# First head group of a fused attention and MLP kernel: two query quarters take their heads in pairs, four tokens load on ScalarE's queue, queries are made three units ahead, two Wo tiles move to empty MLP slots

## The chip, the cores and the metric

The kernel runs on one core of one Trainium2 chip. A core has TensorE (PE, with its weight loads as PEld), VectorE (DVE), ScalarE (ACT), GpSimd (POOL) and SyncE (SP), each with its own instruction queue; DMA transfers are issued from SP, ACT and POOL. The metric is device microseconds of one execution; lower is better.

## The reference

The input x (2048 tokens, 512 wide) is layer-normalised. One branch is attention with 32 heads of 128 against given key and value caches, the other a gated MLP; the result is x + s * silu(B).

```python
xn = _layernorm(x, axis=-1)
# A: attention
q = (xn @ wq).reshape(B, Sq, H, Dh)            # 32 heads of 128
scores = einsum("bhqd,bhkd->bhqk", q, k_cache) * (Dh ** -0.5)
p = softmax(scores)
s = einsum("bhqk,bhkd->bhqd", p, v_cache) @ wo
# B: MLP
h = gelu(_layernorm(xn) @ w1)
hs = shift_quarters(h) @ w2                    # four column quarters moved by 1, -1, 2, -2 tokens
x1 = xn + hs
g = silu(x1 + gelu(_layernorm(x1) @ w3) @ w4)
out = x + s * g
```

## The kernel before

The 2048 tokens are 16 tiles of 128, or four quarters (qt) of 512. The 32 heads are eight groups (g) of four (hh). A *unit* is one head of one quarter, 128 in all, in the order of the list `units` (line 121): group, then quarter, then head. A unit has eight *steps*; step p of unit u has the number n = 8u + p. The loop from line 695 writes out the order of every engine by hand (`pin` keeps program order):

- `s_slot` (line 183): two score matmuls into one of two buffers `ps_s`, and one exp of 128x1024 on ACT into `pT`.
- `pv_slot` (line 212), five steps later: two matmuls of `pT` with values into `ps_o`.
- `q_mm` and `q_copy` (lines 167, 175): the four matmuls of the query projection of unit u + 2, in steps 0 and 1, and their copy to `qT` on DVE in step 2 (on ACT in the last units).
- DVE adds the exps of a unit into `acc` (`add_first`, `add_next`, `add_last`); `sums` (line 223) reduces it with four narrow matmuls in step 3 of the next unit; the reciprocal goes through DRAM (`dr`) and is broadcast (`rb`) by two SP DMAs; `norm` (line 253) scales `ps_o` into `oT` in step 2 of the unit after that.
- When the four heads of a quarter are done, `wo_todo` gets its four token tiles. One tile a unit: four Wo matmuls in steps 4 and 5 and a DVE add into `s_acc` in step 6.
- The MLP is cut into 136 *chunks* of mostly four matmuls. Steps 2, 3 and 6, 7 are its windows, two a unit, from unit 5 on; a count spreads the chunks evenly, so that some windows stay empty. The first chunks (`gelu_chunk`) put on ACT a PSUM copy each, and a square and a tanh for each pair.

PSUM has two small banks besides: `xa` (queries, sums, Wo) and `xm` (MLP chunks; the sums of the last seven units).

Before the loop, tokens 0 to 3 are normalised, turned on TensorE and copied to `xnT`, two of three ACT copies first, and the first query made (`first_tokens`, line 377). `xnT` for tokens 4 to 15 is made beside the loop: load on POOL's queue (`ln1_load`), statistics on DVE with a root on POOL (`ln1_stats`), normalisation on DVE (`ln1_apply`), and a transposing DMA on SP (`ln1_turn`). The table `tokens` (line 661) gives the step of each. Keys come by transposing DMAs on SP, four pieces a head (`load_k`), values in two halves (`load_v`). DMAs of SP and ACT share eight completion counters, which a scheduler gives out in turn; a DMA whose counter is still held by an earlier one waits on its engine's queue.

Of the kernel before, what the change touches and what calls it, by code (L numbers as in the profile page):

```python
# [10 lines left out]
FP32 = mybir.dt.float32  # L11
# [6 lines left out]
def kernel(  # L18
# [15 lines left out]
    nc = tc.nc  # L34
# [4 lines left out]
    Sq, D = x2d.shape  # L39
# [78 lines left out]
        pin(nc.gpsimd.tensor_scalar(out=ve[:], in0=var, scalar1=EPS, scalar2=None, op0=ALU.add))  # L118
        pin(nc.gpsimd.tensor_tensor(out=out, in0=ve[:], in1=nhalf[:], op=ALU.pow))

    units = [(g, qt, hh) for g in range(NG) for qt in range(QT) for hh in range(HG)]
    NU = len(units)
    QUIET = NU - 7
    LQ = QT - 1
    deferred = {(NG - 2, qt): qt for qt in (LQ - 1, LQ)}
    NS = NU * SPU
    kTs, vBs, wqs, wos, oTs, st = {}, {}, {}, {}, {}, {}
# [2 lines left out]
    def at(n, fn):  # L130
        todo[n].append(fn)
# [6 lines left out]
    def evict(n):  # L138
        return n if n % SPU == SPU - 1 else n + 1

    def load_k(h, pieces):
        w = Sk // KSPLIT
        for i in pieces:
            if i == 0:
                kTs[h] = kp.tile([P, Sk], BF16, name="kT")
            pin(nc.sync.dma_start(
                out=kTs[h][:, i * w:(i + 1) * w],
                in_=A_k_cache[0, h, i * w:(i + 1) * w, :], transpose=True))
# [14 lines left out]
    def load_wo(h):  # L163
        wos[h] = wop.tile([P, D], BF16, name="wo_h")
        pin(nc.sync.dma_start(out=wos[h][:], in_=A_wo[h * Dh:(h + 1) * Dh, :]))

    def q_mm(u, dcs):
        g, qt, hh = units[u]
        if dcs[0] == 0:
            st[u] = dict(psq=psX.tile([P, 512], FP32, tag="xm" if u == HG else "xa", name="ps_q"))  # L170
        for dc in dcs:
            mm(st[u]["psq"][:], wqs[g * HG + hh][:, dc, :],
               xnT[:, dc, qt * 512:(qt + 1) * 512], dc == 0, dc == DC - 1)

    def q_copy(u):
        qT = qtp.tile([P, 512], BF16, name="qT")
        if u > QUIET + 1:
            pin(nc.scalar.activation(out=qT[:], in_=st[u].pop("psq")[:], func=ACT.Identity))
        else:
            pin(nc.vector.tensor_copy(out=qT[:], in_=st[u].pop("psq")[:]))  # L180
        st[u]["qT"] = qT
# [40 lines left out]

    def sums(u):
        s = st[u]
        ps = psX.tile([P, 4], FP32, tag="xa" if u + 1 < QUIET else "xm", name="ps_sum")
        a = s["acc"][:, 0, :].rearrange("k (p j) -> k j p", j=4)
        for j in range(4):
            mm(ps[:, j:j + 1], a[:, j, :], ones_t[:], True, True)
        recip(s, ps)
# [36 lines left out]
    def wo_mm(g, t, hhs):  # L266
        if hhs[0] == 0:
            wo_box[0] = psX.tile([P, D], FP32, tag="xa", name="ps_wo")
        held = g == NG - 1 and (NG - 2, t // 4) in deferred
        if held and hhs[0] == 0:  # L270
            wo_part(wo_box[0][:], g - 1, t, range(HG), True, False)
        wo_part(wo_box[0][:], g, t, hhs, hhs[0] == 0 and not held, hhs[-1] == HG - 1)

    def wo_part(ps, g, t, hhs, first, last):
        oT = oTs[(g, t // 4)]
        ts = t % 4
        for hh in hhs:
            mm(ps, oT[:, hh, ts * P:(ts + 1) * P], wos[g * HG + hh][:],
               first and hh == hhs[0], last and hh == hhs[-1])
# [61 lines left out]
    def ln1_load(t, eng):  # L341
        xin = tokp.tile([P, D], BF16, tag="ta", bufs=8, name="xin")
        pin(eng.dma_start(out=xin[:], in_=xsrc[t]))
        ln[t] = xin
# [21 lines left out]
    def ln1_apply(t):  # L366
        xns[t] = ln1_norm(t)

    def ln1_turn(t):
        pin(nc.sync.dma_start_transpose(out=xnT[:, :, t * P:(t + 1) * P], in_=xns.pop(t)[:]))  # L370
# [273 lines left out]
        ln1_load(t, eng)  # L644
    act1 = const.tile([P, 1], FP32, name="act1")
    pin(nc.scalar.activation(out=act1[:], in_=nhalf[:], func=ACT.Identity))
    for h in range(HG - 1):
        load_w(h, nc.gpsimd)
    load_k(0, range(KSPLIT))
# [3 lines left out]
    for t in range(4):  # L653
        ln1_stats(t)
    load_w(HG - 1, nc.gpsimd)
    for t in range(4, 8):
        ln1_load(t, nc.gpsimd)
    first_tokens()
    load_v(1, (0, 1))
    load_k(2, (0, 1))  # L660
    tokens = ((2, 4, 5), (5, 9, 12), (8, 12, 13), (11, 14, 14),
              (21, 27, 27), (23, 29, 29), (29, 35, 35), (35, 39, 39),
              (39, 45, 45), (47, 53, 53), (55, 61, 61), (63, 69, 69))
    for t, (stats, apply, turn) in enumerate(tokens, 4):
        if t >= 8:
            at(stats - 8, lambda t=t: ln1_load(t, nc.gpsimd))
        at(stats, lambda t=t: ln1_stats(t))
        at(apply, lambda t=t: ln1_apply(t))
        at(turn, lambda t=t: ln1_turn(t))
    for n, h, piece in ((2, 2, 2), (4, 2, 3), (12, 3, 0), (15, 3, 1), (17, 3, 2), (20, 3, 3)):  # L670
        at(n, lambda h=h, piece=piece: load_k(h, (piece,)))
    for n, h, half in ((7, 2, 0), (13, 2, 1), (20, 3, 0), (21, 3, 1)):
        at(n, lambda h=h, half=half: load_v(h, (half,)))
    at(28, ph1_load)
    at(64, w2_load)
    for h in range(HG):
        at(31 + h, lambda h=h: load_wo(h))
    for g in range(NG - 1):
        b = (g * QT + QT - 1) * HG
        for hh in range(HG):  # L680
            h = (g + 1) * HG + hh
            for i in range(KSPLIT):
                at((b - 2 + (2 * hh + i // 2 + (hh > 0))) * SPU + (5, 7)[i % 2], lambda h=h, i=i: load_k(h, (i,)))
            for i in range(2):
                at((b - 2 + (2 * hh + i + (hh > 0))) * SPU + 6, lambda h=h, i=i: load_v(h, (i,)))
            at((b + (-4, -4, -1, -1)[hh]) * SPU + (5, 7)[hh % 2], lambda h=h: load_w(h))
            at((b - 4 - hh // 2) * SPU + (5, 7)[hh % 2], lambda h=h: load_wo(h))

    at(QUIET * SPU, tail_open)
    for t in range(4 * LQ, NT):  # L690
        if t % 4 < 2:
            at((QUIET + 1 + 2 * (t % 4)) * SPU + 4, lambda t=t: gate_sum(t))

    wo_todo = deque()
    for n in range(NS):
        u, p = divmod(n, SPU)
        s_slot(u, p)
        m = n - LAG
        if m >= 0:
            pv_slot(*divmod(m, SPU))  # L700
        if u == 0 and p in (1, 3, 5):
            q_mm(1 + p // 2, range(DC))
        if u == 0 and p in (2, 4, 6):
            q_copy(p // 2)
        if u == HG - 2 and p in (6, 7):
            q_mm(HG, (2 * p - 12, 2 * p - 11))
        if u == HG - 2 and p == 7:
            q_copy(HG)
        if p in (0, 1) and HG - 1 <= u < NU - 2:
            q_mm(u + 2, (2 * p, 2 * p + 1))  # L710
        if p == 0 and u >= 1:
            add_last(u - 1)
        if p == 2 and HG - 1 <= u < NU - 2:
            q_copy(u + 2)
        if p == 2 and u >= 2:
            norm(u - 2)
            gg, qq, hh = units[u - 2]
            if hh == HG - 1 and (gg, qq) in deferred:
                pin(nc.sync.dma_start(out=o_d[qq][:], in_=oTs[(gg, qq)][:]))
            elif hh == HG - 1:  # L720
                wo_todo.extend((gg, 4 * qq + ts) for ts in range(4))
                if gg == NG - 1:
                    fin_load(4 * qq)
        if p == 3 and u >= 1:
            sums(u - 1)
        if p == 4 and u >= 1:
            bcast(u - 1)
        if p in (4, 5) and wo_todo:
            wo_mm(*wo_todo[0], (0, 1) if p == 4 else (2, 3))
        if p == 6 and QUIET <= u < NU - 1:  # L730
            add_next(u, 2)
        if p == 6 and wo_todo:
            gg, t = wo_todo.popleft()
            wo_post(gg, t)
            if gg == NG - 1:
                at(n + 5, lambda t=t: wo_out(t))
                if t % 4 < 3:
                    fin_load(t + 1)
        if p == 4:
            add_first(u)  # L740
        if p == 4 and u == NU - 1:
            a = st[u]["acc"]
            pin(nc.vector.tensor_tensor(out=a[:, 0:2, :], in0=a[:, 0:2, :], in1=a[:, 2:4, :], op=ALU.add))
        if p == 6 and u < QUIET:
            add_next(u, 2)
        if p in (2, 3, 6, 7):
            w = 2 * u + (p >= 4)
            i = p % 2
            if i == 0:
                want = -(-(w + 1 - W0) * NCH // (W1 - W0)) if w >= W0 else 0  # L750
                window.pop("run", None)
                if done < min(want, NCH):
                    if done in hooks:
                        hooks.pop(done)(n)
                    window["run"] = chunks.popleft()
                    done += 1
            if "run" in window:
                window["run"](i, n)
        for fn in todo.pop(n, ()):
            fn()  # L760
# [78 lines left out]
```

## Time and profile before

| what | value |
|---|---|
| median of 3 runs | 1279.92 us (1279.73 to 1281.28) |
| profiled execution, its time | 1279.53 us |
| its span, first to last instruction | 1277.8 us |
| exps (ACT, 128x1024), one after another | 0.92 us each (15 in 13.86 us) |
| first score matmul | 10.29 us |
| units 1 to 4 (18.92 to 52.75) | 33.83 us |
| units 5 to 12 (52.75 to 133.24) | 80.49 us |
| transposing DMAs of keys, issue to landing, median | 4.7 us |
| transposing DMAs of `xnT`, issue to landing, median | 3.8 us |

Times in the text are microseconds from the start of the span unless they are durations. A unit's window runs from its first exp to the next unit's first exp. Matmul ends are modelled in the profile, so the pitch of matmuls is read from their starts and from whole units. A row of the timeline has start, duration, engine, line, operation and tiles, and in brackets the idle time before it and what ended it; a row of the waits has total, times and longest.

### The profile page before, as it was taken

The numbers are of one execution on the slowest core, as the hardware profiler recorded it, in microseconds if no ns is written. First come the engines' busy times: TensorE is split into PE (matmuls) and PEld (weight loads), VectorE is DVE, ScalarE is ACT, GpSimd is POOL, SyncE is SP. The second block draws the span as 40 slices with busy tenths as digits, with TensorE's granted clock in tenths as the row PEclk, the third lists the DMA queues.
The fourth block names the chain that finished last, engine by engine and source line by source line (L and its number), as shares of the span: only waits on it lengthen the run. The fifth ranks groups of instructions, "written<-read, shape, count | busy, mean of one in ns | idle before, by whom it ended". The sixth has DMA issues, their size and how long they took to land.

```text
span 1277.8 us, 17233 instructions
## 1 busy us (share of the span) xinstructions
PE 1257.1 (98%) x6195; PEld 612.1 (48%) x6320; DVE 1019.2 (80%) x1407; ACT 1113.0 (87%) x1195; POOL 137.9 (11%) x241
## 2 busy tenths in 40 slices
PE   8999999999999999999999999999999999999998
PEld 5444444444444444444444444444444444444444
DVE  7888889898788877778887778887777888777886
ACT  7899998888999988899988889998888999888883
POOL 4430003323110010000001000000000000000110
PEclk9999999999999999999999999999999999999999
DMA  9644343455532564134443244523435133542532
GB/s 185 133 106 81 59 79 88 108 124 123 115 77 67 100 110 89 42 75 83 89 93 68 58 85 93 96 42 75 96 80 90 34 70 72 91 105 46 140 76 58
DMA packets 172950, 111.79 MB, mean 87 GB/s; under 512 B 124800, under 2 KB 149888, under 8 KB 172864
## 3 DMA queue, kind: packets, MB, share of 16 engines
q1 hardware_dynamic: 163904, 85.51, 34.3%
q0 software_dynamic: 8672, 24.91, 7.9%
q8 instruction: 49, 0.80, 0.3%
q14 instruction: 37, 0.30, 0.1%
q10 hardware_dynamic: 288, 0.26, 0.1%
HBM read 82.58 MB, written 7.60 MB: 71 GB/s over the span
## 4 chain that ended last, share of the span: by engine, by line
PE 87%; ACT 6%; DVE 4%; issue 1%; DMA 1%; POOL 0%; DVEq 0%; ACTq 0%
PE ps_s L114 31%; PE ps_o L114 30%; PE ps_m L114 9%; PE ps_wo L114 8%; PE ps_q L114 7%; ACT pT L194 4%; PE ps_sum L114 1%; ACT sq L425 1%; DVE acc L205 1%; ACT pre L455 1%; DVE bn L349 0%; DMA rb<-dr 0%; DMA xnT<-xn 0%; DVE acc L210 0%; DVE qT L180 0%
## 5 line engine op out<-in xcount | busy, mean ns | idle before, releaser
L194 ACT ACTIVATE pT<-ps_s 128x1024 bf16<-128x1024 f32 x1024 | 1012.0, 1031 | 141.0 <-PE ps_s L114 130.0
L114 PE MATMUL ps_s<-qT,kT 128*128 128x512 bf16 x2004 | 599.5, 379 | 4.1 <-ACT pT L194 1.0
L114 PE MATMUL ps_o<-pT,vb 128*128 128x512 bf16 x1997 | 597.6, 379 | 2.8
L205 DVE TENSOR_TENSOR acc<-acc,pT 128x2048 bf16<-128x2048 bf16 x254 | 309.8, 1220 | 65.5 <-ACT pT L194 60.8
L114 PEld LDWEIGHTS <-kT 128*128 128x128 bf16 x2048 | 226.8, 113 | 224.4 <-issue 18.6
L114 PEld LDWEIGHTS <-vb 128*128 128x128 bf16 x2048 | 199.8, 98 | 225.2
L200 DVE TENSOR_TENSOR acc<-pT 128x2048 bf16<-128x2048 bf16 x128 | 155.9, 1218 | 26.6 <-ACT pT L194 26.4
L114 PE MATMUL ps_q<-xnT,wq_h 128*128 128x512 bf16 (+1 forms) x519 | 150.7, 374 | 3.3 <-DMA xnT<-xn 2.0
L114 PE MATMUL ps_wo<-wo_h,oT 128*128 128x512 bf16 x456 | 136.3, 379 | 0.6
L328 DVE TENSOR_TENSOR s_acc<-ps_wo,s_acc 128x512 f32<-128x512 f32 x100 | 68.9, 689 | 73.9 <-PE ps_wo L114 71.0
L210 DVE TENSOR_TENSOR acc<-acc 128x1024 bf16<-128x1024 bf16 x127 | 87.9, 692 | 4.4
L261 DVE TENSOR_TENSOR oT<-ps_o,rb 128x512 bf16<-128x512 f32 x129 | 87.1, 676 | 4.1 <-DMA rb<-dr 4.0
L180 DVE CAST qT<-ps_q 128x512 bf16<-128x512 f32 x122 | 83.5, 685 | 4.8 <-PE ps_q L114 4.8
L114 PEld LDWEIGHTS <-wq_h 128*128 128x128 bf16 x524 | 50.6, 98 | 63.2 <-issue 3.6
L114 PEld LDWEIGHTS <-oT 128*128 128x128 bf16 x480 | 46.9, 98 | 57.7 <-issue 2.6
L114 PE MATMUL ps_m<-xn2T,w_sb 128*128 128x512 bf16 x222 | 66.1, 378 | 0.2
L114 PE MATMUL ps_m<-w_sb,h2T 128*128 128x512 bf16 x218 | 62.7, 379 | 0.2
L577 POOL DMA_DIRECT2D w_sb<-in_B_w_dram x28 | 21.1, 756 | 353.8 <-PE ps_m L114 328.6
L211 DVE TENSOR_TENSOR acc<-acc 128x512 bf16<-128x512 bf16 x127 | 54.0, 425 | 4.3
L233 DVE RECIPROCAL rc<-ps_sum 128x4 f32<-128x4 f32 x128 | 22.9, 179 | 40.9 <-PE ps_sum L114 40.0
L114 PEld LDWEIGHTS <-acc 128*128 128x128 bf16 x516 | 37.6, 115 | 29.6 <-issue 1.5
L609 POOL DMA_DIRECT2D g_d<-xr x16 | 8.8, 547 | 346.3 <-DVE xr L607 346.3
(74 smaller groups left out, 599.9 us busy)
## 6 DMA issues: line engine op xcount, KB each, us to landing
rb<-dr SPq DMA_DIRECT2D x128, 256.0 KB, 4.1
vb<-in_A_v_cache_dram SPq DMA_DIRECT2D x64, 256.0 KB, 4.5
w_sb<-in_B_w_dram POOLq DMA_DIRECT2D x28, 256.0 KB, 4.6
wo_h<-in_A_wo_dram SPq DMA_DIRECT2D x32, 128.0 KB, 3.9
wq_h<-in_A_wq_dram SPq DMA_DIRECT2D x28, 128.0 KB, 4.2
kT<-in_A_k_cache_dram SPq DMA_TRANSPOSE x128, 4.7
dr<-rc SPq DMA_DIRECT2D x128, 2.0 KB, 1.4
xr<-in_A_x_dram POOLq DMA_DIRECT2D x16, 128.0 KB, 3.5
```

The source lines that it names most:

```text
L114: pin(nc.tensor.matmul(out=out, lhsT=lhsT, rhs=rhs, start=start, stop=stop))
L180: pin(nc.vector.tensor_copy(out=qT[:], in_=st[u].pop("psq")[:]))
L194: pin(nc.scalar.activation(out=s["pT"][-1][:, jj:jj + 2, :], in_=sps[:], func=ACT.Exp, scale=SCALE))
L200: pin(nc.vector.tensor_tensor(out=s["acc"][:], in0=s["pT"][0][:], in1=s["pT"][1][:], op=ALU.add))
L205: pin(nc.vector.tensor_tensor(out=a[:], in0=a[:], in1=st[u]["pT"][i][:], op=ALU.add))
L210: pin(nc.vector.tensor_tensor(out=a[:, 0:2, :], in0=a[:, 0:2, :], in1=a[:, 2:4, :], op=ALU.add))
L211: pin(nc.vector.tensor_tensor(out=a[:, 0, :], in0=a[:, 0, :], in1=a[:, 1, :], op=ALU.add))
L233: pin(nc.vector.reciprocal(out=rc[:], in_=ps[:]))
L261: pin(nc.vector.tensor_tensor(out=oTs[(g, qt)][:, hh, c], in0=s["o"][:, c], in1=s["rb"][:, c], op=ALU.mult))
L328: pin(nc.vector.tensor_tensor(out=sa, in0=ps[:], in1=sa, op=ALU.add))
L425: pin(nc.scalar.activation(out=sq[:], in_=pre[:], func=ACT.Square, scale=GELU_A ** 0.5))
L577: pin(nc.gpsimd.dma_start(out=w[:], in_=w3_v[:, :, fc * P:(fc + 2) * P]))
```

## The change

- `units`: in group 0, quarters 0 and 1 take heads 0 and 1 first (quarter 0, then quarter 1), then heads 2 and 3; after that the order is as before. Heads 2 and 3 are first used in units 4 and 5 and no longer in units 2 and 3; quarter 1 is first used in unit 2 and no longer in unit 4.
- Tokens 4 to 7 are loaded on ACT's queue ahead of `first_tokens` and no longer on POOL's; their statistics, normalisations and transposes stand in steps 0 to 7. The key, value, w1 and Wo loads of the first units get other steps.
- `q_mm` and `q_copy` run three units ahead (`QL`), with a table of their own for the first units. In the last units the queries use bank `xm` and the sums `xa`, the other way round than before.
- In units 8 and 9, whose second MLP window is empty, `wo_extra` runs a further Wo tile there, with a copy on DVE.

```diff
--- before.py
+++ after.py
@@ -118,10 +118,13 @@
         pin(nc.gpsimd.tensor_scalar(out=ve[:], in0=var, scalar1=EPS, scalar2=None, op0=ALU.add))
         pin(nc.gpsimd.tensor_tensor(out=out, in0=ve[:], in1=nhalf[:], op=ALU.pow))
 
-    units = [(g, qt, hh) for g in range(NG) for qt in range(QT) for hh in range(HG)]
+    units = [(0, qt, hh) for h0 in (0, 2) for qt in (0, 1) for hh in (h0, h0 + 1)]
+    units += [(0, qt, hh) for qt in range(2, QT) for hh in range(HG)]
+    units += [(g, qt, hh) for g in range(1, NG) for qt in range(QT) for hh in range(HG)]
     NU = len(units)
     QUIET = NU - 7
     LQ = QT - 1
+    QL = 3
     deferred = {(NG - 2, qt): qt for qt in (LQ - 1, LQ)}
     NS = NU * SPU
     kTs, vBs, wqs, wos, oTs, st = {}, {}, {}, {}, {}, {}
@@ -167,14 +170,14 @@
     def q_mm(u, dcs):
         g, qt, hh = units[u]
         if dcs[0] == 0:
-            st[u] = dict(psq=psX.tile([P, 512], FP32, tag="xm" if u == HG else "xa", name="ps_q"))
+            st[u] = dict(psq=psX.tile([P, 512], FP32, tag="xm" if u >= QUIET + QL else "xa", name="ps_q"))
         for dc in dcs:
             mm(st[u]["psq"][:], wqs[g * HG + hh][:, dc, :],
                xnT[:, dc, qt * 512:(qt + 1) * 512], dc == 0, dc == DC - 1)
 
     def q_copy(u):
         qT = qtp.tile([P, 512], BF16, name="qT")
-        if u > QUIET + 1:
+        if u >= QUIET + QL:
             pin(nc.scalar.activation(out=qT[:], in_=st[u].pop("psq")[:], func=ACT.Identity))
         else:
             pin(nc.vector.tensor_copy(out=qT[:], in_=st[u].pop("psq")[:]))
@@ -222,7 +225,7 @@
 
     def sums(u):
         s = st[u]
-        ps = psX.tile([P, 4], FP32, tag="xa" if u + 1 < QUIET else "xm", name="ps_sum")
+        ps = psX.tile([P, 4], FP32, tag="xa", name="ps_sum")
         a = s["acc"][:, 0, :].rearrange("k (p j) -> k j p", j=4)
         for j in range(4):
             mm(ps[:, j:j + 1], a[:, j, :], ones_t[:], True, True)
@@ -270,6 +273,16 @@
         if held and hhs[0] == 0:
             wo_part(wo_box[0][:], g - 1, t, range(HG), True, False)
         wo_part(wo_box[0][:], g, t, hhs, hhs[0] == 0 and not held, hhs[-1] == HG - 1)
+
+    def wo_extra(g, t):
+        def run(i, n):
+            if i == 0:
+                mlp["ps"] = psX.tile([P, D], FP32, tag="xm", name="ps_m")
+            wo_part(mlp["ps"][:], g, t, (2 * i, 2 * i + 1), i == 0, i == 1)
+            if i == 1:
+                ps = mlp["ps"]
+                at(evict(n), lambda: pin(nc.vector.tensor_copy(out=s_acc[:, t, :], in_=ps[:])))
+        return run
 
     def wo_part(ps, g, t, hhs, first, last):
         oT = oTs[(g, t // 4)]
@@ -644,6 +657,8 @@
         ln1_load(t, eng)
     act1 = const.tile([P, 1], FP32, name="act1")
     pin(nc.scalar.activation(out=act1[:], in_=nhalf[:], func=ACT.Identity))
+    for t in range(4, 8):
+        ln1_load(t, nc.scalar)
     for h in range(HG - 1):
         load_w(h, nc.gpsimd)
     load_k(0, range(KSPLIT))
@@ -653,28 +668,24 @@
     for t in range(4):
         ln1_stats(t)
     load_w(HG - 1, nc.gpsimd)
-    for t in range(4, 8):
-        ln1_load(t, nc.gpsimd)
     first_tokens()
     load_v(1, (0, 1))
-    load_k(2, (0, 1))
-    tokens = ((2, 4, 5), (5, 9, 12), (8, 12, 13), (11, 14, 14),
-              (21, 27, 27), (23, 29, 29), (29, 35, 35), (35, 39, 39),
-              (39, 45, 45), (47, 53, 53), (55, 61, 61), (63, 69, 69))
-    for t, (stats, apply, turn) in enumerate(tokens, 4):
+    tokens = ((0, 3), (1, 4), (2, 5), (3, 7), (17, 21), (21, 23), (23, 29), (27, 31),
+              (39, 45), (45, 53), (53, 55), (55, 61))
+    for t, (stats, apply) in enumerate(tokens, 4):
         if t >= 8:
-            at(stats - 8, lambda t=t: ln1_load(t, nc.gpsimd))
+            at(stats - 6, lambda t=t: ln1_load(t, nc.gpsimd))
         at(stats, lambda t=t: ln1_stats(t))
-        at(apply, lambda t=t: ln1_apply(t))
-        at(turn, lambda t=t: ln1_turn(t))
-    for n, h, piece in ((2, 2, 2), (4, 2, 3), (12, 3, 0), (15, 3, 1), (17, 3, 2), (20, 3, 3)):
-        at(n, lambda h=h, piece=piece: load_k(h, (piece,)))
-    for n, h, half in ((7, 2, 0), (13, 2, 1), (20, 3, 0), (21, 3, 1)):
-        at(n, lambda h=h, half=half: load_v(h, (half,)))
+        at(apply, lambda t=t: (ln1_apply(t), ln1_turn(t)))
+    for h, slots, halves in ((2, (9, 10, 13, 14), (16, 18)), (3, (22, 24, 25, 26), (30, 32))):
+        for i, n in enumerate(slots):
+            at(n, lambda h=h, i=i: load_k(h, (i,)))
+        for i, n in enumerate(halves):
+            at(n, lambda h=h, i=i: load_v(h, (i,)))
     at(28, ph1_load)
     at(64, w2_load)
     for h in range(HG):
-        at(31 + h, lambda h=h: load_wo(h))
+        at(40 + h, lambda h=h: load_wo(h))
     for g in range(NG - 1):
         b = (g * QT + QT - 1) * HG
         for hh in range(HG):
@@ -683,7 +694,7 @@
                 at((b - 2 + (2 * hh + i // 2 + (hh > 0))) * SPU + (5, 7)[i % 2], lambda h=h, i=i: load_k(h, (i,)))
             for i in range(2):
                 at((b - 2 + (2 * hh + i + (hh > 0))) * SPU + 6, lambda h=h, i=i: load_v(h, (i,)))
-            at((b + (-4, -4, -1, -1)[hh]) * SPU + (5, 7)[hh % 2], lambda h=h: load_w(h))
+            at((b + (-5, -5, -2, -2)[hh]) * SPU + (5, 7)[hh % 2], lambda h=h: load_w(h))
             at((b - 4 - hh // 2) * SPU + (5, 7)[hh % 2], lambda h=h: load_wo(h))
 
     at(QUIET * SPU, tail_open)
@@ -691,6 +702,10 @@
         if t % 4 < 2:
             at((QUIET + 1 + 2 * (t % 4)) * SPU + 4, lambda t=t: gate_sum(t))
 
+    early_q = {1: (1, range(DC)), 3: (4, range(DC)), 5: (5, range(DC)),
+               13: (2, (0, 1)), 14: (2, (2, 3)), 16: (3, (0, 1)), 17: (3, (2, 3)),
+               24: (6, (0, 1)), 25: (6, (2, 3))}
+    early_copy = {2: 1, 4: 4, 6: 5, 15: 2, 18: 3, 26: 6}
     wo_todo = deque()
     for n in range(NS):
         u, p = divmod(n, SPU)
@@ -698,20 +713,16 @@
         m = n - LAG
         if m >= 0:
             pv_slot(*divmod(m, SPU))
-        if u == 0 and p in (1, 3, 5):
-            q_mm(1 + p // 2, range(DC))
-        if u == 0 and p in (2, 4, 6):
-            q_copy(p // 2)
-        if u == HG - 2 and p in (6, 7):
-            q_mm(HG, (2 * p - 12, 2 * p - 11))
-        if u == HG - 2 and p == 7:
-            q_copy(HG)
-        if p in (0, 1) and HG - 1 <= u < NU - 2:
-            q_mm(u + 2, (2 * p, 2 * p + 1))
+        if n in early_q:
+            q_mm(*early_q[n])
+        if n in early_copy:
+            q_copy(early_copy[n])
+        if p in (0, 1) and 4 <= u < NU - QL:
+            q_mm(u + QL, (2 * p, 2 * p + 1))
         if p == 0 and u >= 1:
             add_last(u - 1)
-        if p == 2 and HG - 1 <= u < NU - 2:
-            q_copy(u + 2)
+        if p == 2 and 4 <= u < NU - QL:
+            q_copy(u + QL)
         if p == 2 and u >= 2:
             norm(u - 2)
             gg, qq, hh = units[u - 2]
@@ -754,6 +765,8 @@
                         hooks.pop(done)(n)
                     window["run"] = chunks.popleft()
                     done += 1
+                elif p == 6 and u in (8, 9):
+                    window["run"] = wo_extra(*wo_todo.popleft())
             if "run" in window:
                 window["run"](i, n)
         for fn in todo.pop(n, ()):
```

## Prediction

> **What bounds the kernel now.** I read the page first, then the waits of TensorE, then busy time unit by unit. (A unit is one head of one 512-query quarter: eight steps of two score matmuls, one exp and two PV matmuls.)
>
> ```profile
> span 1277.8 us, 17233 instructions
> PE 1257.1 (98%) x6195; PEld 612.1 (48%) x6320; DVE 1019.2 (80%) x1407; ACT 1113.0 (87%) x1195; POOL 137.9 (11%) x241
> ```
>
> TensorE is busy 98% of the span. Matmuls are fixed in number by the computation, so only idle time, or time in which another engine paces TensorE, can be won. The waits of TensorE are short and few:
>
> ```profile
> PE ps_q L114 <- DMA xnT<-xn: 2.0, 1, 2.0
> PE ps_q L114 <- DVE s_acc L328: 0.8, 2, 0.5
> PE ps_sum L114 <- DVE qT L180: 0.6, 2, 0.4
> ```
>
> The first is the one this change is aimed at; the second is two waits near the end. Next, windows that begin and end at the first exp of a unit: units 2, 5, 6, 12, 123 and 125 (length, then PE, PEld, DVE, ACT, POOL busy with counts, clock, DMA share, GB/s):
>
> ```profile
> 26.18:36.34 10.16, 8.15 (x40) 3.79 (x40) 6.90 (x11) 7.63 (x10) 2.69 (x4) 1.00 0.91 161
> 52.75:63.87 11.12, 10.64 (x53) 5.13 (x53) 9.09 (x16) 9.12 (x12) 3.40 (x6) 1.00 0.44 83
> 63.87:73.72 9.85, 9.74 (x49) 4.69 (x49) 9.07 (x13) 9.80 (x13) 1.90 (x2) 1.00 0.19 54
> 123.62:133.24 9.62, 9.57 (x49) 4.68 (x49) 7.05 (x11) 8.35 (x11) 0.00 (x0) 1.00 0.70 104
> 1214.80:1224.04 9.24, 8.73 (x45) 4.29 (x45) 7.53 (x11) 8.14 (x11) 1.08 (x2) 1.00 0.32 73
> 1232.82:1242.91 10.09, 9.74 (x49) 4.69 (x49) 7.55 (x11) 8.25 (x11) 1.08 (x2) 1.00 0.41 80
> ```
>
> Unit 12 has 44 matmuls of 512 columns by the code and takes 9.62 us. With 0.13 us for its four short sum matmuls that is 0.2157 us a matmul, the pitch used below. Unit 6 has the same 44 but takes 9.85, and there ScalarE is busy 9.80: eight exps plus a PSUM copy, a square and a tanh. So a unit costs the larger of its matmuls at 0.2157 and ScalarE's work.
>
> **Part 1, tokens 4 to 7 on ScalarE's queue.** In the start, with SyncE's row of the second K piece and its landing:
>
> ```profile
> 7.49 1.08 ACT L400 ACTIVATE xnT<-ps_o 128x512 bf16<-128x512 f32 x2 [4.35 <-PE ps_o L114]
> 8.78 0.60 ACT L400 ACTIVATE xnT<-ps_s 128x512 bf16<-128x512 f32 x1 [0.20 <-PE ps_s L114]
> 10.29 1.03 PE L114 MATMUL ps_s<-qT,kT 128*128 128x512 bf16 x3 [0.47 <-DVE qT L415]
> ...
> L146 SPq DMA_TRANSPOSE kT<-in_A_k_cache_dram x1: 1251/1251/1251, 2.9 to 2.9; - x1
> DMA to landing us min/median/max: 6.7/6.7/6.7
> ```
>
> The instruction order of the changed program puts four more DMA issues on ScalarE ahead of these copies, and the fourth has a wait:
>
> ```
> L356 DMACopy xin_212<-in_A_x_dram 128x512 [waits DMAHW5_49]
> L413 Activation xnT_58<-ps_o_319 128x4x128 [waits PE_49]
> ```
>
> DMAs from SyncE and ScalarE share eight completion counters in turn; counter 5 belongs first to head 0's second K piece, issued at 2.9 and landed 6.7 later, at 9.6. The first three loads wait for tokens 0, 2 and 3, long landed. So ScalarE is held to 9.6, plus 0.45 for the issue (its two issues at the start take 0.90): 10.05. Behind it stand the three xnT copies and most of the first qT. From the first copy to the first score matmul the rows have 10.29 - 7.49 = 2.80, of which 0.20 was ScalarE waiting for TensorE; 2.60 remain. The first score matmul moves from 10.29 to 12.65: **+2.4 us**. ScalarE idled there 4.35 us before; that cover ends at 7.49, and the rest is paid.
>
> [...] The trace agrees for SyncE, whose queue stood 168.5 us in 119 broadcasts until the DMA before had landed; no row shows it on ScalarE.
>
> The three early loads (0.39 MB) now also run against that K piece. Lower bound 0, since the DMA queues moved 160 GB/s in the first 10 us and 249 in the next; upper bound 0.39 MB at 160 GB/s = 2.5. I take 0.4, near the lower end, because the piece is on SyncE's queue and not behind these loads. Start: **+2.8** (0 to 4.9).
>
> SyncE moves with it: vb(0)'s second half waits for the first K piece (7.6) and head 1's first K piece for the third piece of head 0 (issued 4.19, 5.6 to land: 9.8 against an issue at 7.94 before). They shift 1.9 us and the steps that need them 2.8: covered.
>
> **Part 2, pairs of heads, units 1 to 4.** Before, these four took 18.92 to 52.75 = 33.8 us, and hold the 2.0 wait: the transposes of tokens 4 to 7 stood on SyncE behind head 2's four K pieces. Now each unit has 36 matmuls and sums, 36 x 0.2157 + 0.13 = 7.9, or 31.6 in all, four matmuls more than before. Exps alone need 8 x 0.92 = 7.4 and do not bind. VectorE nearly does: three adds of 1.2, the two folds (0.7, 0.4), qT and oT copies (0.6 each) and 0.1 are 6.0 a unit; unit 2 gets three statistics (0.8) and two normalisations (0.3) besides, 9.1 against 7.9, ahead of the add that its sums matmul needs. Bounds of VectorE's lateness over these units: 0 (unit 4's slack of 1.9 absorbs it) and 2.4 (1.2 twice, units 0 and 2). I take 1.1, the middle. Units 1 to 4: 32.7, **-1.1**.
>
> New wait: tokens 4 to 7 feed q of unit 2 at step 13. VectorE, from qT at 12.5 + 0.4: four statistics 3.2, three qT copies 1.9, four normalisations 1.3, two adds 2.4 make 21.7. Landing took 2.5, 5.0, 3.5 and 4.3 in the four old ones, up to 6.2 in all twelve: 24.2 to 27.9. Step 13 comes 8.0 (unit 0) + 5 x 0.92 + 0.9 after 13.05, at 26.5. Wait 0 to 1.4; I take **+0.3**. Queued behind it on TensorE are unit 2's first scores.
>
> **Part 3, Wo tiles, units 5 to 12.** Before 133.24 - 52.75 = 80.5. Now unit 5 loses four Wo matmuls: 44, 9.6. Unit 6 has 40, but ScalarE's 9.8 keeps it at 9.8, so nothing is won. Unit 7 stays 9.85. Units 8 and 9 get four each: 48 x 0.2157 + 0.13 = 10.5 each. Units 10 to 12 stay (10.55, 9.85, 9.62). Sum 80.3: **-0.2** (bounds -0.6, +0.8: unit 5's 0.4 wait for VectorE may stay or move to unit 7).
>
> **Part 4, queries three ahead, at the end.** q moves to the xm bank in the last units, so it no longer waits for the Wo sum on xa: the waits of 0.51 and 0.30 go, -0.8. The sums take xa instead, three steps after that read ended: 0. Unit 125 loses its q, four matmuls, -0.86 (they are the four more of part 2). ScalarE's eight exps, 7.4, stay below its 8.8. **-1.65.** In between, q is only shifted from u + 2 to u + 3, and weights load one unit earlier on an unfilled SyncE queue: 0; a buffer wait there would cost some 0.4 a group.
>
> **Sum.** 2.8 - 1.1 + 0.3 - 0.2 - 1.65 = +0.15: span 1278.0, the profiled execution 1279.53 + 0.15 = 1279.7; the median of the runs is 0.4 above that execution, so **1280.1 us**, no change. What a measurement can tell here is 0.2%, 2.6 us; its own range is 1277.6 to 1282.5.
>
> **Rivals.**
> - *ScalarE is not held* (or the K piece lands by 7): part 1 is 0, time 1277.3. For it: no ScalarE row shows a queue wait. Against: every SyncE issue behind a wait stands in order. Chance 0.17.
> - *The start's DMA queue is the bound*: the early loads push the gating K piece back by their whole 2.5 us, to 12.1, and the transposes of tokens 4 to 7 land late too, 2.0 rather than 0.3: 1280.1 + 2.1 + 1.7 = 1283.9. It decides from a landing at about 11.5. For it: 249 GB/s at a 1.19 share of the engines in 10 to 20 us. Against: 0.96 and 160 GB/s before that. Chance 0.25.
> - *VectorE takes the wait's place*: 2.4 rather than 1.1 in units 1 to 4, and 0.5 more in unit 7: 1281.9. For it: unit 6 has VectorE busy 9.07 of 9.85; against: unit 2 had 3.3 us free. Chance 0.10, nearly all of it inside 0.2%.
> - The forecast: 0.48.
>
> **Numbers.** Faster 0.18 (the first rival), slower 0.26 (the second, and a little of the third), same 0.56. Leaving out half of each outer rival gives 1277.0 to 1283.8.
>
> **What would show it.** In the changed profile ScalarE's first xnT copy stands near 10 rather than 7.5 and the first score matmul near 12.7 to 13; the 2.0 wait is gone and at most 0.3 of it is left at step 13; unit 6 is unchanged, units 8 and 9 take 10.5; the two waits on s_acc near the end are gone. A first copy at 7.5 makes part 1 wrong; waits of the sums on VectorE above 1.5 in units 1 to 4 make part 2 wrong.

## The result, and the profile after

The changed kernel takes 1284.39 us (median of 7 runs, 1283.61 to 1284.78) against 1279.74 for the one before (7 runs beside them): ratio 1.0032, 95% interval 1.0021 to 1.0044. It is slower, by more than the 0.2% that can be told here, and it lies 0.6 above the upper end of the range. The profiled execution took 1284.78, its span is 5.2 us longer than before's.

The page of the changed kernel:

```profile
span 1283.0 us, 17360 instructions
PE 1266.0 (99%) x6320; PEld 612.8 (48%) x6320; DVE 1020.1 (80%) x1408; ACT 1113.4 (87%) x1194; POOL 135.5 (11%) x237
```

TensorE's share went up, but the two traces can't be compared by it: before's holds 6195 matmul records and this one 6320. Records of 512 columns last 0.379 us here at a pitch of 0.2157, so where one is missing a hole of some 0.05 us is left; by that estimate 125 of them are some 6 us, most of the 8.9 between the two. The kernel below with three edits together, with 6320 records and without the half clock in the start, has 1264.4 us busy, so a small part of the 1266.0 is a clock that was halved. A higher share is no better use here. The waits of TensorE (total, times, longest):

```profile
PE ps_q L114 <- ACT xnT L413: 3.2, 1, 3.2
PE ps_sum L114 <- DVE qT L183: 1.8, 2, 1.1
PE ps_o L114 <- DVE oT L264: 1.2, 1, 1.2
```

The wait of 2.0 for `xnT` and the two waits for `s_acc` are gone, as the change meant. In their place stand a wait of 3.2 ahead of the first query, two waits of sums for VectorE (1.1 in unit 3, 0.66 in unit 7), and one for `oT` in unit 4. ScalarE in the start, by the timeline (start, duration, then the row):

```profile
3.44 7.82 ACTq L356 DMA_DIRECT2D xin<-in_A_x_dram  x4
11.30 1.08 ACT L413 ACTIVATE xnT<-ps_o 128x512 bf16<-128x512 f32 x2 [8.16 <-DMA xin<-in_A_x_dram]
13.49 0.49 ACT L426 ACTIVATE qT<-ps_q 128x384 bf16<-128x384 f32 x1 [0.61 <-PE ps_q L114]
```

The four issues occupy ScalarE's queue for 7.82 us. By the records of the trace three of them are over at 4.94; the fourth waits until 10.92, ends at 11.26, and only then comes the first copy to `xnT`, at 7.49 before. The fourth issue, and SyncE's first two key pieces by their DMAs:

```profile
L356 ACTq DMA_DIRECT2D xin<-in_A_x_dram x1: 335/335/335, 10.9 to 10.9; - x1
...
L149 SPq DMA_TRANSPOSE kT<-in_A_k_cache_dram x2: 1229/1237/1245, 1.6 to 2.9; - x2
DMA to landing us min/median/max: 5.9/7.0/8.0
```

The second of them, issued at 2.9, is the one that took 8.0: landed at 10.90, where before it landed at 9.57. In this trace and in those of the six kernels below that have the four single loads and the hold, the fourth issue starts 0.01 to 0.02 us after that piece has landed, whether it landed at 9.66 or at 11.37. The trace of the changed kernel has the semaphores too: the DMAs of SyncE's and ScalarE's queues tell their landing by eight of them, the completion counters (71 or 72 of the 574 DMAs each). The fourth issue waits for number 107, that of this key piece (landed at 10.90, issue at 10.92), the three ahead of it for those of tokens 0, 2 and 3 (landed at 3.42, 4.05 and 4.29). TensorE in the same stretch:

```profile
11.95 1.93 PE L114 MATMUL ps_q<-xnT,wq_h 128*128 128x128 bf16 x16 [3.17 <-ACT xnT L413]
14.36 1.87 PE L114 MATMUL ps_s<-qT,kT 128*128 128x512 bf16 x4 [0.47 <-DVE qT L428]
```

The first score matmul moved from 10.29 to 14.36. Four score matmuls took 1.87 us. Four take 1.03 in an experiment below, and so do those of before, whose row has three records for the four. The reason is in the windows (length, then PE, PEld, DVE, ACT, POOL busy with counts, clock, DMA share, GB/s):

```profile
8.79:11.95 3.16, 0.00 (x0) 0.00 (x0) 0.14 (x1) 0.65 (x2) 0.00 (x0) 0.85 1.11 197
11.95:14.36 2.41, 1.93 (x17) 1.63 (x17) 0.44 (x2) 1.42 (x3) 0.00 (x0) 0.50 1.11 295
14.36:17.82 3.46, 3.46 (x9) 1.27 (x10) 1.39 (x4) 1.94 (x2) 1.56 (x4) 0.50 0.74 105
15.41:24.57 9.16, 8.93 (x36) 3.90 (x35) 6.91 (x14) 7.53 (x8) 4.17 (x9) 0.87 0.68 146
...
40.97:50.22 9.25, 8.15 (x42) 3.89 (x41) 8.36 (x15) 7.65 (x10) 5.81 (x15) 1.00 0.94 128
50.22:59.53 9.31, 8.06 (x42) 3.81 (x40) 6.47 (x9) 7.67 (x9) 0.00 (x0) 1.00 0.86 177
...
89.30:99.69 10.39, 10.39 (x53) 4.98 (x52) 8.63 (x11) 10.09 (x13) 0.54 (x1) 1.00 0.72 184
1221.85:1230.63 8.78, 8.78 (x46) 4.29 (x45) 7.55 (x11) 8.14 (x10) 0.88 (x3) 1.00 0.35 75
1239.41:1248.41 9.00, 9.00 (x46) 4.21 (x45) 7.46 (x11) 7.59 (x10) 1.35 (x3) 1.00 0.45 96
```

The granted clock, 1.00 everywhere in the windows shown of before, is 0.50 from 10.99 for 6.83 us, after the idle stretch of 3.17. Over the whole execution the clock was 0.996 or 0.997 in all seven runs of the changed kernel. Unit 0 (15.41 to 24.57) takes 9.16 where it took 8.00. The other rows are units 3, 4, 8, 123 and 125. Put together by the first exps of units:

| stretch | before | after | difference | predicted |
|---|---|---|---|---|
| start and unit 0 | 18.92 | 24.57 | +5.66 | +2.8 |
| units 1 to 4 | 33.83 | 34.95 | +1.1 | -1.1, and +0.3 for `xnT` |
| units 5 to 12 | 80.49 | 80.72 | +0.2 | -0.2 |
| unit 13 to the end | 1144.5 | 1142.8 | -1.75 | -1.65 |

The wait in unit 4 has a chain of its own. SyncE's queue, then VectorE at its end:

```profile
43.77 5.15 SPq L149 DMA_TRANSPOSE kT<-in_A_k_cache_dram  x3
48.96 0.58 SPq L238 DMA_DIRECT2D dr<-rc  x1
50.62 0.32 SPq L253 DMA_DIRECT2D rb<-dr  x1
```

```profile
55.90 0.69 DVE L264 TENSOR_TENSOR oT<-ps_o,rb 128x512 bf16<-128x512 f32 x1 [2.50 <-DMA rb<-dr]
```

The reciprocal of unit 2 was made at 46.28, but its way through DRAM was issued at 48.96, behind three key pieces; the broadcast `rb` landed at 55.9, and TensorE, which needs the bank that `oT` is read from, waited 1.25 us. This wait varies between executions and kernels with the same steps here: 1.24, 1.36 and 2.82 in three kernels below, 0.21 in another. In unit 3 VectorE is the late one: ahead of the last fold of unit 2 (the last add that halves its `acc`) it had three statistics and two normalisations to do, and the second normalisation stood 0.78 us for GpSimd's root:

```profile
41.64 0.41 DVE L367 TENSOR_SCALAR xn<-xin,mv,rs 128x512 bf16<-128x512 bf16 x1 [0.78 <-POOL rs L119]
41.97 0.69 DVE L362 BATCH_NORM_STATS2 bn<-xin 128x6 f32<-128x512 bf16 x1
...
44.74 0.43 DVE L214 TENSOR_TENSOR acc<-acc 128x512 bf16<-128x512 bf16 x1
```

The sums of unit 2, made in unit 3, wait for that fold: TensorE stands from 44.72 to 45.82.

### The profile page after: what moved, and what is told of

Same layout as the page of the kernel before. It is cut to its first block, busy times and chain, and to the rows that moved or that the text cites. A ratio compares the mean times of both kernels' runs of the same rounds, so it can differ in the third digit from the quotient of the medians.

```text
span 1283.0 us, 17360 instructions
## 1 busy us (share of the span) xinstructions
PE 1266.0 (99%) x6320; PEld 612.8 (48%) x6320; DVE 1020.1 (80%) x1408; ACT 1113.4 (87%) x1194; POOL 135.5 (11%) x237
## 4 chain that ended last, share of the span: by engine, by line
PE 89%; ACT 6%; DMA 2%; DVE 1%; SPq 1%; issue 0%; POOL 0%; DVEq 0%; ACTq 0%
PE ps_s L114 32%; PE ps_o L114 31%; PE ps_m L114 9%; PE ps_wo L114 8%; PE ps_q L114 7%; ACT pT L197 4%; ACT sq L438 1%; PE ps_sum L114 1%; DMA xin<-in_A_x_dram 1%; ACT pre L468 1%; DMA dr<-rc 0%; DMA rb<-dr 0%; SPq L149 0%; DMA wo_h<-in_A_wo_dram 0%; DVE acc L208 0%
## 5 line engine op out<-in xcount | busy, mean ns | idle before, releaser
L114 PE MATMUL ps_s<-qT,kT 128*128 128x512 bf16 x2048 | 609.6, 379 | 2.4 <-ACT pT L197 1.0
L114 PE MATMUL ps_o<-pT,vb 128*128 128x512 bf16 x2048 | 608.6, 379 | 1.2 <-DVE oT L264 1.2
L114 PE MATMUL ps_q<-xnT,wq_h 128*128 128x512 bf16 (+1 forms) x524 | 153.4, 379 | 3.2 <-ACT xnT L413 3.2
```

Of the source, the lines that this page charges most:

```text
L114: pin(nc.tensor.matmul(out=out, lhsT=lhsT, rhs=rhs, start=start, stop=stop))
```

## The experiments

In all of them the time of before, run beside them, was 1280.0 to 1280.2. "Unit 13" is the time of its first exp: 133.24 before, 140.25 in the changed kernel. From there on the two differ only in the last units.

### The loads of tokens 4 to 7 back on GpSimd's queue

```diff
-    for t in range(4, 8):
-        ln1_load(t, nc.scalar)
...
     load_w(HG - 1, nc.gpsimd)
+    for t in range(4, 8):
+        ln1_load(t, nc.gpsimd)
     first_tokens()
```

> The changed kernel with the loads of tokens 4 to 7 back on POOL's queue, behind the last query weight; all else changed. Theory A (the hold of ScalarE by the fourth load's counter, and the half clock that follows the gap, make the start dear): ScalarE's first xnT copy back at 7.5 us, first score matmul at 10.3, granted clock 1.00 all through, unit 0 in 8.0 us; about 5.7 of the 1284.4 us go, less up to 1.5 for tokens 4 to 7 that now come late for step 13: 1278.7 to 1280.2. Theory B (the loss lies in units 1 to 4: VectorE and SyncE are overfilled by the new order): the start shrinks but the waits grow in step, time 1282.5 to 1284.4.

1282.70, ratio 1.0021 (1.0012 to 1.0031); unit 13 at 136.96. The first score matmul is back from 14.36 to 11.55, so the loads on ScalarE's queue hold it, but a part of the loss stays, and the time is where the second theory has it: the clock was 0.50 from 7.88 to 11.29 in this execution, after an idle stretch of 1.78 us behind the warm-up matmuls, queries in unit 0 waited 0.43 and 0.19 for VectorE, and the waits of units 3, 4 and 7 (1.09, 1.24, 0.69) are all there.

### Two loads of two tokens each on ScalarE's queue

```diff
+    def ln1_load2(t, eng):
+        xin = ph1.tile([P, 2, D], BF16, name=f"xin{t}")
+        pin(eng.dma_start(out=xin[:], in_=xsrc[t:t + 2].rearrange("t p d -> p t d")))
+        ln[t], ln[t + 1] = xin[:, 0, :], xin[:, 1, :]
...
-    for t in range(4, 8):
-        ln1_load(t, nc.scalar)
+    for t in (4, 6):
+        ln1_load2(t, nc.scalar)
```

> The changed kernel with tokens 4 to 7 still on ScalarE's queue at the same place and with the same bytes, but as two loads of two tokens: they take the counters of the first token loads, and no load waits for a key piece. Theory A: first xnT copy at 7.5, first score matmul at 10.3 to 10.6, clock 1.00, 1278.5 to 1279.5. Rival C (the bytes in the DMA queues at the start are the cost, not the counter): the first score matmul still comes at 12 or later, for want of keys or weights, and the time stays above 1282.

1281.28, ratio 1.0009 (1.0000 to 1.0018); unit 13 at 136.89. The same bytes on the same queue at the same place, but in two issues, and neither waits for the key piece. ScalarE of this kernel:

```profile
3.56 0.98 ACTq L361 DMA_DIRECT2D xin<-in_A_x_dram  x2
7.65 1.08 ACT L418 ACTIVATE xnT<-ps_o 128x512 bf16<-128x512 f32 x2 [4.49 <-PE ps_o L114]
```

The queue is held 0.98 us rather than 7.82, the copy stands at 7.65 (7.49 before), the first score matmul at 10.45, and the clock stays at 1.00. So the fourth issue's wait makes the hold, not the bytes or the place of the loads. The key piece does land later with them:

```profile
L149 SPq DMA_TRANSPOSE kT<-in_A_k_cache_dram x1: 1250/1250/1250, 2.9 to 2.9; - x1
DMA to landing us min/median/max: 8.0/8.0/8.0
```

It lands as late as in the changed kernel (10.87), but here ScalarE doesn't wait for it. In the eleven traces with early loads on ScalarE's queue it landed at 9.66 to 11.37, in the three without at 8.77 to 9.57. The rest of the loss is elsewhere: unit 4 waits 2.8 us for `rb` in this one, and the time lies between the two expectations.

### Dummy matmuls in the idle stretch

```diff
@@ first_tokens, behind the transposes of the four tokens
+        warm_up(40)
```

> The changed kernel with 40 more 128-column matmuls on the identity between the turns of the first tokens and the first query, where TensorE sat idle for 3.2 us; the hold stays. If the gap halves the clock: clock 1.00 throughout, first copies still at 11.3, unit 0 in 8.0 rather than 9.2 us, and 1.2 to 1.8 us less in all, 1282.6 to 1283.2. If the slow unit 0 has another cause (VectorE's statistics, the keys), unit 0 stays above 9 and the time is 1284.4.

1283.28, ratio 1.0025 (1.0015 to 1.0034). ScalarE is held at least as long as in the changed kernel (the copy stands at 11.77), but the idle stretch is 0.87 us. The window of unit 0:

```profile
14.90:22.90 8.00, 7.70 (x36) 3.62 (x35) 7.43 (x16) 7.53 (x9) 4.39 (x10) 1.00 0.97 153
```

The clock is 1.00 (0.999 or 1.000 over the whole execution in all nine runs) and unit 0 takes 8.00, 1.17 less than in the changed kernel. The first score matmuls stand at 14.26 all the same, and four of them take 1.03. The median is 1.1 below the changed kernel's, 0.9 by the ratios: what the half clock costs there, less what the dummies and the later copy cost. The intervals of the two ratios overlap.

### Only the loads, in the kernel before

```diff
@@ the kernel before
+    for t in range(4, 8):
+        ln1_load(t, nc.scalar)
...
-    for t in range(4, 8):
-        ln1_load(t, nc.gpsimd)
```

> The kernel before with one part of the change alone: tokens 4 to 7 loaded on ScalarE's queue ahead of the first copies, everything else as it was. Theory A: the fourth load waits for the second key piece, first xnT copy near 11, half clock after it, first score matmul near 14; the time rises by 4 to 6 us to 1283.7 to 1285.7 (the 2.0 us wait for xnT in unit 2 may shrink). Theory B: the start is hidden by the waits that follow, 1279.7 to 1281.

1284.09, ratio 1.0035 (1.0021 to 1.0049): this part alone costs before 3.9 us.

```profile
3.91 6.11 ACTq L343 DMA_DIRECT2D xin<-in_A_x_dram  x4
10.06 1.08 ACT L400 ACTIVATE xnT<-ps_o 128x512 bf16<-128x512 f32 x2 [6.91 <-DMA xin<-in_A_x_dram]
```

In this execution the copy stands at 10.06, where the prediction put it (10.05), and the clock was still halved for 6.83 us from 9.75 on: first score matmul at 13.11, unit 0 at 9.16. The early tokens shorten the 2.0 wait for `xnT` to 1.4 and no more.

### Key pieces later

```diff
-    for h, slots, halves in ((2, (9, 10, 13, 14), (16, 18)), (3, (22, 24, 25, 26), (30, 32))):
+    for h, slots, halves in ((2, (12, 13, 14, 21), (16, 22)), (3, (24, 28, 29, 31), (32, 36))):
```

> The changed kernel with the key and value loads of heads 2 and 3 at other steps, so that no key piece stands on SyncE's queue between the transposes of unit 2 and the sums' DMA of unit 3; tokens 8 to 15 as changed, the hold of ScalarE stays. If the wait of PV in unit 4 (1.25 us, on oT, on the broadcast of sums) comes from SyncE's queue: that wait gone, unit 4 in about 8.0 us, the waits of 1.10 (unit 3) and 0.66 (unit 7) unchanged, and 1.2 us less in all, 1283.2. If the broadcast is late because VectorE made the sums late, the wait stays above 0.8 and the time is 1284.4.

1284.41, ratio 1.0031 (1.0019 to 1.0043). Unit 4 has no wait any more (7.99), so its 1.25 came from SyncE's queue; but a wait of 1.34 of the same kind stands in unit 5, which takes 11.16. The waits of units 3 and 7 are as they were.

```profile
PE ps_o L114 <- DVE oT L264: 1.3, 1, 1.3
```

### Statistics of tokens 8 to 15 at other steps

```diff
-    tokens = (... (17, 21), (21, 23), (23, 29), (27, 31), (39, 45), (45, 53), (53, 55), (55, 61))
+    tokens = (... (12, 15), (14, 20), (20, 23), (27, 30), (37, 40), (41, 45), (57, 59), (59, 63))
```

> The changed kernel with the statistics and normalisations of tokens 8 to 15 at other steps (1 of the 5 statistics of units 2 and 3 less in unit 2, none in unit 6); key loads as changed, the hold stays. If the waits of the sums in units 3 and 7 (1.10 and 0.66) are VectorE's fill: both under 0.2, units 3 and 7 in 8.0 and 9.8; 1.7 us less, 1282.7, and up to 1.2 more where the earlier sums let the broadcast in unit 4 come in time. If they come from the exps or from POOL's root, they stay.

1284.17, ratio 1.0036 (1.0022 to 1.0050). The wait in unit 3 falls from 1.1 to 0.39 and the one in unit 7 from 0.66 to 0.34: both were VectorE's. A new wait of 0.95 comes at the end of unit 1, where the scores of unit 2 wait for their query, whose copy now stands behind the statistics of tokens 8 and 9. The wait was moved.

### The three together, and with the hold put back

```diff
@@ the changed kernel with the three edits: double loads, later key pieces, other steps
...
@@ and a second kernel, the same but for
-    for t in (4, 6):
-        ln1_load2(t, nc.scalar)
+    for t in range(4, 8):
+        ln1_load(t, nc.scalar)
```

> The two-token loads on ScalarE's queue, the key loads of the run with keys later and the steps of the run with tokens spread, together: the change with its three new waits taken away. If the three account for what the change lost: first score matmul at 10.3 to 10.6, no wait over 0.5 in units 1 to 7, unit 13 begins near 132.3 rather than 140.3, and 1276.2 to 1277.5 us, 0.2 to 0.3% less than before. If there is a fourth cause (ScalarE's pace, or a shift of the same wait to xnT at step 13), it stays at 1279 or above.

> As the run with all three, but the loads of tokens 4 to 7 on ScalarE's queue one by one again, as changed: only the hold is back. If costs add up, 3.1 to 4.3 us over the run with all three, 1279.5 to 1281.5; the first copy at 11.3, half the clock for one stretch. If the hold was hidden behind the other waits, or they behind it, the difference is under 2.

Together: 1279.68, ratio 0.9994 (0.9986 to 1.0003), unit 13 at 134.95. With the four single loads: 1283.18, ratio 1.0022 (1.0012 to 1.0032), unit 13 at 140.01. So the hold with its half clock costs 3.5 us by the medians, with nothing else changed. The three edits do not bring the expected 1276.2 to 1277.5: it stays above 1279, as with a fourth cause. Unit 2's query is 0.94 late, as with the steps alone, and there is a wait of 1.39 us in unit 0, which the kernel with the hold does not have: the last query weight, issued at 7.86 by GpSimd behind the roots, lands 9.3 later:

```profile
17.24 1.04 PE L114 MATMUL ps_q<-xnT,wq_h 128*128 128x512 bf16 x4 [1.39 <-DMA wq_h<-in_A_wq_dram]
```

### Two steps of that kernel, and a third

```diff
@@ the three together
-    tokens = (... (12, 15), (14, 20), (20, 23), (27, 30), ...
+    tokens = (... (17, 20), (20, 23), (25, 28), (28, 31), ...
-    early_q = {1: (1, range(DC)), 3: (4, range(DC)), 5: (5, range(DC)),
+    early_q = {1: (1, range(DC)), 3: (4, range(DC)), 7: (5, range(DC)),
-    early_copy = {2: 1, 4: 4, 6: 5, 15: 2, 18: 3, 26: 6}
+    early_copy = {2: 1, 4: 4, 8: 5, 15: 2, 18: 3, 26: 6}
@@ and a second kernel, the same but for
-    tokens = (... (17, 20), (20, 23), (25, 28), (28, 31), ...
+    tokens = (... (17, 20), (20, 25), (26, 29), (29, 33), ...
```

> The kernel with two double loads, later key pieces and spread tokens (e7), with two more steps changed: the query of unit 5, which needs the last query weight, is made at step 7 and no longer at step 5, and the statistics of tokens 8 to 11 stand at steps 17, 20, 25 and 28, none of them ahead of unit 2's query copy. Theory (the excess is made of waits at named places, which add up): the 1.39 us wait for the weight and the 0.94 us wait of unit 2's scores for qT go, nothing new above 0.5 us appears, unit 0 takes 8.2 and unit 13 starts near 132.7, where before has 133.24; with the 1.75 us of the end the time is 2.3 below e7: 1277.4, ratio to before 0.998. Rival (VectorE has no room in units 1 to 4 for tokens 4 to 11 in any order, so a wait removed comes back at another place, as it did when the key pieces or the tokens alone were moved): a wait of a sums matmul for VectorE of about 1 us in units 2 to 4, unit 13 near 134 and the time 1278.5 to 1279.7.

> The last kernel (e9) with the normalisation of token 9 moved from step 23 to step 25 and tokens 10 and 11 at steps 26 to 29 and 29 to 33. In e9 unit 3 waits 1.1 us for VectorE, which in unit 2 had stood 0.77 us for GpSimd's root ahead of that normalisation (0.41). Theory (the wait hangs on those 1.18 us): the wait of unit 3 goes, none above 0.4 us comes in unit 4, unit 13 starts near 133.0 and the time is 1.1 below e9: ratio to before 0.999. Rival (VectorE's room in units 1 to 4 is used up, a wait removed comes back): about 1 us of waits for VectorE or for token 11's transpose in units 4 and 5, unit 13 near 134 and the ratio 0.9998 as for e9.

The first: 1279.76, ratio 0.9998 (0.9989 to 1.0007). The waits for the weight and in unit 2 are gone, but unit 3 waits 1.1 for VectorE again; unit 13 at 134.11, the time as without the edit. Unit 3 of this kernel:

```profile
35.92:45.16 9.24, 8.09 (x41) 3.87 (x41) 8.04 (x14) 7.65 (x9) 3.27 (x6) 1.00 0.97 130
```

The second: 1280.35, ratio 1.0001 (0.9992 to 1.0009). Unit 3 now takes 8.06, without a wait; unit 4 waits 1.34 for VectorE and unit 5, whose query needs token 11 turned, 1.70 for a DMA; unit 13 at 135.53. Both went as the rival said: a wait taken away in this group comes back one unit later.

### The banks of the last units, in the kernel before

```diff
@@ the kernel before
-            ... tag="xm" if u == HG else "xa", name="ps_q"
+            ... tag="xm" if u == HG or u >= QUIET + 2 else "xa", name="ps_q"
-        ps = psX.tile([P, 4], FP32, tag="xa" if u + 1 < QUIET else "xm", name="ps_sum")
+        ps = psX.tile([P, 4], FP32, tag="xa", name="ps_sum")
```

> Before, with the change of banks at the end alone: queries of the last units in xm, all sums in xa. Theory: the two waits of a query for s_acc (0.51 and 0.30 us) are gone, no other wait comes, units 123 and 125 are 0.5 and 0.3 shorter, the start is as before, and the time is 0.8 below before: ratio 0.9994. Rival: the waits pass to the sums in xa, which then stand behind the Wo copy: ratio 1.0000, with waits of ps_sum for s_acc near 1215 and 1233.

1279.15, ratio 0.9994 (0.9985 to 1.0002). The waits of queries for `s_acc` are gone and none came for the sums; unit 123 takes 8.78 (9.24 before) and unit 125 9.63 (10.09), 0.46 each, 0.9 together. That agrees with the expected 0.8, but the interval includes no change. By the way this execution showed something of before that its own profile does not. Unit 2's wait for `xnT` was 2.34 long here, 1.96 there (windows ahead of and behind its end):

```profile
31.21:34.62 3.41, 1.07 (x6) 0.34 (x5) 1.99 (x4) 1.59 (x2) 2.26 (x3) 1.00 1.28 197
34.62:38.03 3.41, 3.19 (x9) 1.21 (x9) 0.23 (x1) 1.02 (x1) 0.00 (x0) 0.50 0.26 70
```

The clock was halved for 3.41 us after it, and unit 2 took 12.24 rather than 10.16.

### A shorter idle stretch

```diff
@@ first_tokens of the changed kernel
+        warm_up(8)
```

> The changed kernel with 8 dummy matmuls behind the tokens' turns, where the earlier one had 40: TensorE's idle stretch ahead of the first query should be 2.4 to 2.8 us long, between the 3.17 that halved the granted clock for 6.83 us and the 0.87 that did not; in profiles of before, 2.0 in unit 2 left it at 1.00, and in one of e10 2.34 halved it for some 3.4 us. Theory (the length of the idle stretch decides, with the bound between 2.0 and 2.34): the clock falls to 0.50 in unit 0, for 3.4 or 6.8 us, unit 0 takes 8.6 to 9.2 and the time is 1283.8 to 1284.4. Rival (an idle stretch under 3.1 costs no clock, and e10's drop had another cause): clock 1.00 through unit 0, which takes 8.0, and the time 1283.2 as with 40.

1283.18, ratio 1.0021 (1.0010 to 1.0032). The stretch did not come out as planned: in this execution the key piece landed earlier, the copy stood at 10.63 and TensorE idled only 1.35 us. The clock was halved all the same:

```profile
8.93:12.34 3.41, 1.76 (x26) 1.39 (x24) 0.34 (x1) 1.57 (x3) 0.05 (x1) 1.00 1.20 189
12.34:15.75 3.41, 2.93 (x11) 1.09 (x10) 1.84 (x5) 1.92 (x3) 1.55 (x4) 0.50 1.05 255
```

So neither bound of the expectations holds: 1.35 us of idle time among narrow matmuls came ahead of a half clock, 1.96 among wide ones did not. The length of the idle stretch does not part these two; the columns counted in the last section do. The seven runs lie between 1281.03 and 1284.93.

## Why the prediction was wrong

**Part 1, the start: the step that failed.** "Start: +2.8 (0 to 4.9)" was +5.66 with unit 0, the largest error of the sum, 2.9 of 5. Its mechanism was right: ScalarE is held at its fourth issue until the second key piece lands (the kernel with two double loads has no hold, and the four issues in the kernel before have one). That this wait stands in ScalarE's own queue, on which the +2.4 rests and which no row of before showed, is in the changed kernel's trace: 7.82 us in the queue's row, and the first copy starts at 11.30, 0.04 after the fourth issue has ended. Two sizes were off:
- *The landing.* "held to 9.6" took the landing from before, and 0.4 was added for the bytes, near the lower end of 0 to 2.5, "because the piece is on SyncE's queue and not behind these loads". The piece landed at 10.90, 1.3 later, though it is on another queue: by these traces the loads delayed it (8.77 to 9.57 in three traces without them, 9.66 to 11.37 in eleven with them). The first copy stood at 11.30, 3.81 later than before and not 2.56; less the 0.20 that ScalarE no longer waits for TensorE, the hold cost 3.6. In the other kernels with the hold the copy stood at 10.06 to 11.77, so that this term also has a spread of more than 1 us between executions.
- *The clock, which no term held.* The prediction moved 2.60 us of work to a later time at its old speed. The held stretch left TensorE idle, the clock fell to 0.50 for 6.83 us, and the moved work itself became longer: 0.46 from the first copy to the first score matmul (3.06, not 2.60), 0.42 from there to the first exp, 1.17 in unit 0; 2.05 in all, and 3.61 + 2.05 = 5.66. The experiment with 40 dummies supports it: unit 0 at 8.00 with the clock at 1.00.

**Part 2, units 1 to 4: wrong in sign.** "Units 1 to 4: 32.7, -1.1" was 34.95, +1.1. The prediction's 31.6 of matmuls lacks two things.
- Waits of 2.35: 1.10 of VectorE in unit 3, as much as the 1.1 that was taken, and 1.25 in unit 4 through SyncE, which the prediction gave no term: `dr` and `rb` are issued on the same queue behind the moved key pieces, here behind three that stood in a row for 5.15 us. With the pieces elsewhere, unit 4 takes 7.99.
- 1.0 of pace. Units 1 and 2, without such waits, take 8.2 and not 7.9. "Exps alone need 7.4 and do not bind" holds for a unit but not for a step: in unit 1 the exps start 0.90 to 0.92 apart in the steps without a query (two score and two PV matmuls are 0.86), and 1.24 and 1.29 in those with two query matmuls (1.29). That this is ScalarE's pace is read from the timeline and was not tried by itself.

`xnT` for unit 2 was in time, so the +0.3 was not there. That is not owed to the late start alone: in the kernel with two double loads, whose first score matmul stands at 10.45, the fourth transpose landed at 23.28, earlier than the 24.2 to 27.9 of the prediction, and unit 2 does not wait for it either.

**Part 3, units 5 to 12.** -0.2 was +0.2. Units 8 and 9 took 10.38 and 10.49 (10.5 predicted). Unit 6 took 9.62, not 9.8, so it did gain a little from its lost matmuls. Unit 7 took 10.40, not 9.85: VectorE's wait of 0.66 had moved there from unit 5, which the bounds named.

**Part 4, the end.** -1.65 was -1.75, and the kernel with the banks alone gave 0.9 for its two waits in the windows.

**The rivals.** That ScalarE is not held fell. The start's queue as the bound came nearest in time (1283.9), and half of its mechanism was there: the loads pushed the key piece back by 1.3 and not 2.5 (to 10.9, not 12.1), but tokens 4 to 7 were turned in time. That it lies within 0.5 of the measured time is luck, since the half clock and the waits for SyncE and VectorE make up the rest. VectorE in place of the wait was there in units 3 and 7, beside SyncE. Even the upper bound of part 1, 4.9, was under the 5.66, since it was made of landings alone.

**What the change could have brought.** Without the hold and with other steps the kernel is equal to before (ratios 0.9994 to 1.0001 in three versions). Part 4 gives 1.75, but 0.86 of it is four matmuls that moved to units 1 to 4, and the wait of 2.0 was replaced by waits of 1.1 to 3 in the same group, whatever step was moved. No version tried is faster by more than can be told. What VectorE and SyncE would need to be free of those waits stays open.

## What to carry to other kernels

A DMA issued on a compute engine's queue held that engine's work here until an unrelated transfer had landed, by way of a completion counter that the two share: 7.82 us of ScalarE's queue, until a key piece of SyncE's had landed at 10.90. So count the DMAs that are issued ahead of it, and make it fewer, larger ones rather than more: two issues for four took 3 us off (1281.28 against 1284.39). An added idle stretch of TensorE is to be priced twice, for its length and, where few columns are streamed around it, for a slower clock behind it: the 3.17 us here were followed by 6.83 at 0.50, and the work from the first copy to the end of unit 0 took 2.05 longer. In a stretch in which VectorE and the DMA engines were both nearly full (8.0 to 8.4 us of 9.2 and a share of 0.94 to 0.97 in two versions of unit 3), moving a step moved the wait; the sum over the group is what to compare, not the one wait that is gone.

## What the runs showed of the hardware

Up to 1255 us, the half clock came for 3.41 us (the loads on GpSimd's queue, later key pieces, the banks, the shorter stretch) or for 6.83 (the changed kernel, the loads alone, the statistics at other steps, the hold put back). In the changed kernel it also came near the end, and its starts there, 10.99 and 1280.75, lie 372 times 3.4133 apart. So I divided each execution, from such a start, into pieces of 3.41 and counted the columns that the matmuls begun in each piece stream (512, 128 or 1 each, from the traces of all 14 kernels here, up to 1255 us): the twelve pieces ahead of a halved one have 896 to 2944, the other 5120 have 3072 or more, of about 8100 that fit at full clock (512 in 0.2157 us). In the changed kernel the two ahead of a halved one, from 7.58 and 10.99 on, have 1152 and 2560, all others from 4.16 on 3584 or more. Before's unit 2 has 3072 recorded in the piece of its 2.0 wait (from 31.99 on), and the hole of one more matmul at 34.63, and the clock stayed at 1.00; the execution with the wait of 2.34 has 2560 in its piece, and the clock was halved behind it.

That the count decides is my reading of these traces and was not tried by itself. If it does, the same idle time is more likely to halve the clock among narrow matmuls than among wide ones, and it matters where in a piece it falls. A matmul at the edge of a piece changes a count by 128 or 512, and three of the traces lack 125 of 6320 matmul records, so the counts are known to a few hundred columns.
